# Attention over the 32 best keys and a feed-forward: values stationary in TensorE, scores in two halves, the mask applied to the scores, the last tokens of two batches merged

## The chip, the core and the metric

The kernel runs on one core of a Trainium2 chip. TensorE (PE) multiplies matrices into PSUM; VectorE (DVE), ScalarE (ACT) and GpSimd (POOL) work on tiles of 128 partitions, GpSimd on SBUF alone; SyncE (SP) issues most of the DMAs. The metric is the device time in microseconds of one execution.

## The reference, cut to what matters

```
B, H, S, D = 8, 8, 576, 64
scores = scale * matmul(q, k^T)                      # 576 x 576 for each of 64 heads
kth    = the 32nd largest of each row
scores = where(scores >= kth, scores, -1e9)
attn   = exp(scores - max);  attn /= sum(attn) + 1e-9
x      = matmul(attn, v)      # (B,H,S,D) -> (4608, 512), the heads side by side
h      = x @ w_in             # 512 -> 2048
out    = (h - tanh(h)) @ w_out  # 2048 -> 512
```

All is float32; the weights arrive as float64 words and are rounded to float32 in the kernel.

## The kernel before, in words

The 576 queries of a batch are four blocks of 128 and a remainder of 64. A *step* is two score tiles of 128 rows and 576 columns: one block of queries in two heads or, for the remainder, 64 queries in four heads, two stacked in a tile. A batch has 18 steps, 16 full and 2 of the remainder; the whole run has 144. Steps go block by block, and in a block through the heads.

For each step four things happen, in three neighbouring rounds of the loop at L378. `scores` (L177) multiplies on TensorE: a matmul of 512 keys and one of 64 for a head, then the same for the other head. Two heads share a tile of 128 partitions, so one head's operands lie on partitions 0 to 63 and the other's on 64 to 127. ScalarE copies the result to `sc` (L191). `top` (L194) finds the 32 largest of each row on VectorE in four rounds: MAX8 takes eight (L202), MATCH_REPLACE strikes them out (L213). After the first round ScalarE already forms the exponentials `e` (L208). After the last, GpSimd compares the scores with the 32nd largest (L216) and multiplies the result into `e` (L219). `weigh` (L221) transposes `e` on TensorE (L227, L233), has ScalarE copy it to `et`, and multiplies it with the values (L247): `et` is stationary, 128 queries wide, and 64 values with a column of ones move, which gives the row sums too.

When all heads of a block are done, `seam` (L262) divides by the sums and transposes the block into `xT` (L281), which is 320 or 256 tokens wide: a *unit* is blocks 0 and 1 of a batch, or 2, 3 and the remainder. The feed-forward of a unit is 64 matmuls with w_in (L298), sixteen tanh (L306) and subtractions (L308), and 16 matmuls of 512 columns with w_out for each block (L318); the remainder's 64 tokens are a block of their own. The source deals this work out over the steps, some 10% faster than it comes in.

Each engine runs its instructions in a fixed order, which a scheduler writes when the program is built: it does not keep the order of the source but moves instructions of neighbouring steps past one another where no data forbid it. PSUM holds one set of scores (four banks), two banks for transposes and values (`zt_ps`), two for the feed-forward (`h_ps`). In the first 13 rounds the weights are converted, 32 pieces of four VectorE, two ScalarE and two GpSimd instructions (L106 to L126). In the built program each matmul of the source is two instructions on TensorE, each transpose one.

Of the kernel before, what the change touches and what calls it, by code (L numbers as in the profile page):

```python
# [14 lines left out]
NEG = -3.0e38  # L15
TOP = 32
# [4 lines left out]
class Block:  # L21
# [3 lines left out]
    def __init__(self, b, qt, H):  # L25
        self.b, self.qt = b, qt
        self.rem = qt == J
        tiles = [(h, h + 1) for h in range(0, H, 2)] if self.rem else [(h,) for h in range(H)]
        self.pairs = [tiles[i : i + 2] for i in range(0, len(tiles), 2)]
        self.xs = None  # L30


class Unit:
    """The tokens of some blocks of one batch, which go through the feed-forward together."""

    def __init__(self, b, qts):
        self.b, self.qts = b, qts
        self.xT = None
        self.g = {}
# [3 lines left out]
def kernel(  # L43
# [16 lines left out]
    DE = D + 1  # L60
# [5 lines left out]
    assert CD == FJ == 4 and DFF // WJ == DM == 512  # L66
    assert D == 64 and R == 64 and DM == H * D
# [8 lines left out]
    ldpool = pool("ld", 2)  # L76
    kqpool = pool("kq", 5)
    scpool = pool("sc", 2)
    wpool = pool("w", 3)
    mpool = pool("m", 16)  # L80
    epool = pool("e", 2)
    etpool = pool("et", 2)
    xpool = pool("x", 2)
    hpool = pool("h", 2)
# [14 lines left out]
    def load_weights(j, i):  # L99
        """Piece i of quarter j (w_in's, then w_out's)."""  # L100
# [8 lines left out]
        # the mantissa: 1 + (its upper 20 bits + its lower 32 bits / 2^32) / 2^20  # L109
# [5 lines left out]
        # the power of two, 0 below float32's range and infinite above it, and the sign  # L115
# [13 lines left out]

    raw, kT, qT, vb = {}, {}, {}, {}  # L130

    def load_rows(dst, src, b, hp):
        for hh in range(2):
            h = 2 * hp + hh
            nc.sync.dma_start(
                dst(slice(0, P), slice(0, J), hh),
                src[b, h, 0:JP, :].rearrange("(p j) d -> p j d", j=J),
            )
            nc.sync.dma_start(dst(slice(0, R), J, hh), src[b, h, JP:S, :])

    def load_kq(b, hp):
        for name, src in (("k", k), ("q", q)):
            t = ldpool.tile([P, J + 1, 2, D], FP32, tag=f"{name}in", name=f"{name}in")
            load_rows(lambda p, j, hh, t=t: t[p, j, hh, :], src, b, hp)
            raw[name, b, hp] = t

    def load_v(b, hp):
        t = kqpool.tile([P, 2, J + 1, DE], FP32, tag="vb", name="vb")
        nc.gpsimd.memset(t[:, :, :, D:DE], 1.0)
        load_rows(lambda p, j, hh: t[p, hh, j, 0:D], v, b, hp)  # L150
        vb[b, hp] = t

    def turn_kq(b, hp):
        for name, dst in (("k", kT), ("q", qT)):
            t = raw.pop((name, b, hp))
            d = dst[b, hp] = kqpool.tile([P, S], FP32, tag=f"{name}T", name=f"{name}T")
            ps = zt_ps.tile([P, 512], FP32, tag="zt", name="kqps")
            for c in range(J):
                nc.tensor.transpose(
                    ps[:, c * P : (c + 1) * P], t[:, c, :, :].rearrange("p h d -> p (h d)"), ident[:]  # L160
                )
            nc.scalar.copy(d[:, 0:JP], ps[:])
            ps = zt_ps.tile([P, 512], FP32, tag="zt", name="kqps")
            nc.tensor.transpose(
                ps[:, 0:R], t[0:R, J, :, :].rearrange("p h d -> p (h d)"), ident[0:R, 0:R]
            )
            nc.scalar.copy(d[:, JP:S], ps[:, 0:R])
# [210 lines left out]
    for n in range(-5, NS + 2):  # L378
        if 0 <= n + 1 < NS:
            scores(n + 1, *steps[n + 1])  # L380
# [51 lines left out]
```

## Time and profile before

| | |
|---|---|
| median of 3 runs | 2315.93 us (2315.67 to 2323.74) |
| the profiled execution, its span (first to last instruction); no other time of it is given | 2319.4 us |
| TensorE matmuls busy | 2118.6 us, 91% |
| VectorE busy | 1630.6 us, 70% |
| GpSimd busy | 1035.6 us, 45% |
| ScalarE busy | 862.4 us, 37% |

Times of a stretch count from the start of the span. A matmul's busy time includes a tail in which the next one already runs, so the pace of a series, its length over its count, is what an instruction costs TensorE; the mean duration is longer. PE rows name the part of the array used, rows x columns: 64*128 is half of its rows.

### The profile page before, as it was taken

The page shows a single profiled execution, that of the slowest core. Times are in us where ns is not written, and L with a number is a line of the kernel's source. Part 1 is how long each engine was busy: PE and PEld are TensorE (multiplying, and loading weights), DVE is VectorE, ACT ScalarE, POOL GpSimd, SP SyncE. Part 2 cuts the span into 40 slices and gives each one's busy share as a digit, 9 for nine tenths or more (in the row PEclk, how much of TensorE's full clock was granted, in tenths as well). Part 3 has the DMA queues.
Part 4 walks back from the last instruction along what each step waited for, and adds up shares of the span by engine and source line. Part 5 has one row for each costly group of instructions (what it writes and reads, how often), then busy time and mean ns, then how long its engine had stood idle before and what let it go on. Part 6 is the DMA issues. An engine that isn't in the chain of part 4 may idle for free.

```text
span 2319.4 us, 26938 instructions
## 1 busy us (share of the span) xinstructions
PE 2118.6 (91%) x9728; PEld 1355.2 (58%) x9728; DVE 1630.6 (70%) x3304; ACT 862.4 (37%) x1825; POOL 1035.6 (45%) x614
## 2 busy tenths in 40 slices
PE   5546688999989999999989999999989999999989
PEld 2334545656656575656656575656556575656654
DVE  5877785767758777777668677767758777767720
ACT  4333333434344344434344344434344344434320
POOL 5656553444434434444434434444434444444420
PEclk6555886999979999999979999999979999999989
DMA  6111102000020001100020001100020001000000
GB/s 166 48 55 55 37 23 50 17 10 3 16 56 1 9 3 43 29 10 3 15 56 1 10 3 46 26 10 3 16 56 1 10 3 38 8 6 7 5 5 12
DMA packets 126724, 56.27 MB, mean 24 GB/s; under 512 B 117888, under 2 KB 117888, under 8 KB 126592
## 3 DMA queue, kind: packets, MB, share of 16 engines
q1 hardware_dynamic: 121984, 37.78, 6.6%
q10 hardware_dynamic: 4608, 16.78, 2.2%
q8 instruction: 77, 1.26, 0.2%
q14 instruction: 55, 0.45, 0.1%
HBM read 45.09 MB, written 9.44 MB: 24 GB/s over the span
## 4 chain that ended last, share of the span: by engine, by line
PE 72%; POOL 10%; DVE 10%; issue 5%; ACT 2%; DMA 1%; SPq 0%; POOLq 0%; ACTq 0%
PE ops L318 24%; PE hps L298 20%; PE av L247 13%; PE scps L183 8%; DVE w L213 4%; PE zt L227 4%; DVE m L202 4%; POOL sc L216 3%; POOL e L219 3%; POOL f L120 2%; ACT sc L191 2%; PE zt L233 1%; DVE f L123 1%; PE xtps L281 1%; DMA kin<-in_k_dram 1%
## 5 line engine op out<-in xcount | busy, mean ns | idle before, releaser
L216 POOL TENSOR_SCALAR sc<-sc,m 128x576 f32<-128x576 f32 x288 | 500.1, 1747 | 986.9 <-DVE m L202 914.5
L202 DVE MAX8 m<-w 128x8 f32<-128x576 f32 x864 | 614.0, 747 | 0.0
L318 PE MATMUL ops<-w_out,g 128*128 128x512 f32 (+1 forms) x1280 | 593.0, 604 | 3.4 <-POOL w_out L126 3.4
L298 PE MATMUL hps<-xT,w_in 128*128 128x320 f32 (+1 forms) x2048 | 549.2, 422 | 6.2 <-DVE g L308 5.1
L298 PEld LDWEIGHTS hps<-xT,w_in 128*128 128x128 f32 x2048 | 393.0, 197 | 125.1 <-issue 20.8
L247 PEld LDWEIGHTS av<-vb,et 128*128 128x128 f32 (+3 forms) x3200 | 400.6, 191 | 98.7 <-issue 22.4
L247 PE MATMUL av<-vb,et 128*128 128x65 f32 (+3 forms) x3200 | 445.1, 284 | 14.0 <-ACT et L230 11.7
L213 DVE MATCH_REPLACE8 w<-m,w 128x576 f32<-128x576 f32 x576 | 427.7, 742 | 0.0
L202 DVE MAX8 m<-sc 128x8 f32<-128x576 f32 x288 | 204.4, 748 | 283.0 <-ACT sc L191 283.0
L219 POOL TENSOR_TENSOR e<-e,sc 128x1152 f32<-128x1152 f32 x144 | 378.7, 2630 | 11.9
L318 PEld LDWEIGHTS ops<-w_out,g 128*128 128x128 f32 (+1 forms) x1280 | 218.3, 181 | 252.9 <-issue 240.9
L183 PE MATMUL scps<-kT,qT 64*128 64x64 f32 (+3 forms) x1280 | 324.9, 480 | 10.9 <-ACT sc L191 10.5
L227 PE MATMUL zt<-ident,e 128*128 128x128 f32 x1152 | 176.5, 300 | 119.2 <-POOL e L219 110.4
L191 ACT COPY sc<-scps 128x1152 f32<-128x1152 f32 x144 | 161.4, 1121 | 326.9 <-PE scps L183 267.9
L306 ACT ACTIVATE th<-hps 128x256 f32<-128x256 f32 (+1 forms) x256 | 105.2, 411 | 372.0 <-PE hps L298 351.3
L183 PEld LDWEIGHTS scps<-kT,qT 64*128 64x128 f32 (+1 forms) x1280 | 139.9, 190 | 160.3 <-issue 132.7
L308 DVE TENSOR_TENSOR g<-hps,th 128x256 f32<-128x256 f32 (+1 forms) x256 | 114.9, 449 | 157.0 <-ACT th L306 156.6
L208 ACT ACTIVATE e<-sc,nb 128x576 f32<-128x576 f32 x288 | 220.8, 775 | 4.2 <-ACT nb L207 0.2
L227 PEld LDWEIGHTS zt<-ident,e 128*128 128x128 f32 x1152 | 138.6, 152 | 133.6 <-POOL e L219 114.9
L213 DVE MATCH_REPLACE8 w<-m,sc 128x576 f32<-128x576 f32 x288 | 211.8, 742 | 0.0
L230 ACT COPY et<-zt 128x512 f32<-128x512 f32 x288 | 157.2, 596 | 13.6 <-PE zt L227 13.5
L255 ACT COPY xs<-av 128x130 f32<-128x130 f32 x144 | 40.2, 279 | 240.6 <-PE av L247 206.7
(45 smaller groups left out, 833.7 us busy)
## 6 DMA issues: line engine op xcount, KB each, us to landing
kin<-in_k_dram SPq DMA_DIRECT2D x64, 128.0 KB, 2.5
raw<-in_moe_w_in_dram ACTq DMA_DIRECT2D x16, 512.0 KB, 4.0
qin<-in_q_dram SPq DMA_DIRECT2D x64, 128.0 KB, 2.5
vb<-in_v_dram SPq DMA_DIRECT2D x64, 128.0 KB, 2.6
raw<-in_moe_w_out_dram ACTq DMA_DIRECT2D x16, 512.0 KB, 3.5
out_dram<-ot SPq DMA_DIRECT2D x32, 256.0 KB, 2.3
kin<-in_k_dram SPq DMA_DIRECT2D x64, 16.0 KB, 2.3
qin<-in_q_dram SPq DMA_DIRECT2D x64, 16.0 KB, 2.3
```

Source lines behind the costliest of these rows:

```text
L183: nc.tensor.matmul(ps[i * R : i * R + ql, ti, s0:s1], qT[g.b, hp][r, g.qt * P : g.qt * P + ql], kT[g.b, hp][r, s0:s1], start=True, stop=True,)
L191: nc.scalar.copy(sc[:], ps[:, :, 0:S])
L202: nc.vector.max(m[ti][:], cur[ti])
L208: nc.scalar.activation(e[:, ti, :], sc[:, ti, :], AF.Exp, bias=nb[:], scale=scale)
L213: nc.vector.match_replace(w[:], m[ti][:], cur[ti], NEG)
L216: nc.gpsimd.tensor_scalar(sc[:, ti, :], sc[:, ti, :], m[ti][:, 7:8], None, ALU.is_ge)
L219: nc.gpsimd.tensor_tensor(e[:], e[:], sc[:], ALU.mult)
L227: nc.tensor.transpose(zt[:, c * P : (c + 1) * P], e[:, ti, c * P : (c + 1) * P], ident[:])
L230: nc.scalar.copy(et[:, ti, 0:J, :], zt[:].rearrange("p (c j) -> p c j", c=J))
L247: nc.tensor.matmul(av[0:ql, nh * DE : (nh + 1) * DE], et[rows, ti, c, i * R : i * R + ql], vb[g.b, hp][rows, h % 2, c, :], start=(c == 0), ...
L298: nc.tensor.matmul(ps[:, 0:N], w_in[j][:, c, fo : fo + P], u.xT[:, c, 0:N], start=(c == 0), stop=(c == CD - 1),)
L318: nc.tensor.matmul(acc[u, qt][0:ql, :], u.g[f][:, o : o + ql], w_out[part][:, f % FJ, :], start=(f == 0), stop=(f == CF - 1),)
```

## The change

Each head pair is now done for two blocks of queries at a time: a batch's steps run through blocks 0 and 1 of the four head pairs, then through blocks 2 and 3, with a remainder step after every second pair. The parts:

- *Scores.* The 576 keys go in two halves of 288. Within a half the two heads follow each other, so the partitions (rows of the array) alternate. The second head's keys are stored with the last 64 first, so that the last 64 of both heads lie side by side in the tile of weights.
- *Mask.* After the search GpSimd forms two numbers per row and head; ScalarE computes a Relu that is 0 for a score among the 32 largest and huge otherwise, GpSimd subtracts it from the scores, and ScalarE takes the exponential of that, which also adds up the row sums. All of it comes after the last round of the search.
- *Weights.* The last 64 keys of both heads are transposed together: nine transposes for ten.
- *Values.* The values (128 keys x 64) are stationary and the transposed weights of two blocks (256 queries) move, so the result comes out transposed, one head in partitions 0 to 63 of `av` (the first 64 columns of the array), the other in 64 to 127. The reciprocals of the sums are spread over 64 columns on GpSimd, transposed on TensorE (`rb`), copied by ScalarE, and VectorE multiplies them into `xT`. `seam` goes.
- *Units.* Blocks 0 and 1, or blocks 2 and 3; in every second batch the second unit also takes the last 64 tokens of two batches as one block, 384 tokens in all.

```diff
+BIG = 2.0**80
...
-    ldpool = pool("ld", 2)
-    kqpool = pool("kq", 5)
+    ldpool = pool("ld", 1)
+    kqpool = pool("kq", 4)
...
+        x = vb[b, hp] = kqpool.tile([P, 2, J, D], FP32, tag="vb", name="vb")
+        y = vr[b, hp] = kqpool.tile([P, D], FP32, tag="vr", name="vr")
+        for t in range(2):
+            h = 2 * hp + t
+            nc.sync.dma_start(x[:, t, :, :], main_rows(v, b, h))
+            nc.sync.dma_start(y[half(t), :], v[b, h, JP:S, :])
...
+            for rows, o in [(half(0), 0), (half(1), R)] if name == "k" else [(slice(0, P), 0)]:
+                nc.scalar.copy(d[rows, o : o + JP], ps[rows, :])
+                o = 0 if o else JP
+                nc.scalar.copy(d[rows, o : o + R], p4[rows, 0:R])
...
+        ps = sc_ps.tile([P, 2, 2, 512], FP32, tag="sc", name="scps")
+        for s in range(2):
+            ks = slice(s * S2, (s + 1) * S2)
+            for i in range(2 if g.rem else 1):
+                qs = slice(JP, S) if g.rem else slice(g.qt * P, (g.qt + 1) * P)
+                rows = half(i) if g.rem else slice(0, P)
+                for t in range(2):
                     nc.tensor.matmul(
-                        ps[i * R : i * R + ql, ti, s0:s1],
-                        qT[g.b, hp][r, g.qt * P : g.qt * P + ql],
-                        kT[g.b, hp][r, s0:s1],
+                        ps[rows, t, s, 0:S2],
+                        qT[g.b, g.hp + i][half(t), qs],
+                        kT[g.b, g.hp + i][half(t), ks],
                         start=True,
                         stop=True,
                     )
-        sc = scpool.tile([P, 2, S], FP32, tag="sc", name="sc")
-        nc.scalar.copy(sc[:], ps[:, :, 0:S])
+        sc = scpool.tile([P, 2, 2, S2], FP32, tag="sc", name="sc")
...
         rounds = TOP // 8
         for i in range(rounds):
-            m = [mpool.tile([P, 8], FP32, tag="m8", name="m8") for _ in range(2)]
-            for ti in range(2):
-                nc.vector.max(m[ti][:], cur[ti])
-            if i == 0:
-                e = epool.tile([P, 2, S], FP32, tag="e", name="e")
-                for ti in range(2):
-                    nb = mpool.tile([P, 1], FP32, tag="nb", name="nb")
-                    nc.scalar.mul(nb[:], m[ti][:, 0:1], -scale)
-                    nc.scalar.activation(e[:, ti, :], sc[:, ti, :], AF.Exp, bias=nb[:], scale=scale)
-                st[n]["e"] = e
+            m8 = slice(8 * i, 8 * i + 8)
+            for t in range(2):
+                nc.vector.max(m[:, t, m8], cur[t])
             if i < rounds - 1:
-                for ti in range(2):
+                for t in range(2):
                     w = wpool.tile([P, S], FP32, tag="w", name="w")
-                    nc.vector.match_replace(w[:], m[ti][:], cur[ti], NEG)
-                    cur[ti] = w[:]
-        for ti in range(2):
-            nc.gpsimd.tensor_scalar(
-                sc[:, ti, :], sc[:, ti, :], m[ti][:, 7:8], None, ALU.is_ge
+                    nc.vector.match_replace(w[:], m[:, t, m8], cur[t], NEG)
+                    cur[t] = w[:]
+        nb = mpool.tile([P, 2], FP32, tag="nb", name="nb")
+        nc.gpsimd.tensor_scalar(nb[:], m[:, :, 0], -scale, None, ALU.mult)
+        tb = mpool.tile([P, 2], FP32, tag="tb", name="tb")
+        nc.gpsimd.tensor_scalar(tb[:], m[:, :, TOP - 1], BIG, None, ALU.mult)
+        z = zpool.tile([P, 2 * S], FP32, tag="z", name="z")
+        zv = z[:].rearrange("p (t k) -> p t k", t=2)
+        den = mpool.tile([P, 2], FP32, tag="den", name="den")
+        for t in range(2):
+            nc.scalar.activation(zv[:, t, :], scf[:, t, :], AF.Relu, bias=tb[:, t : t + 1], scale=-BIG)
+        nc.gpsimd.tensor_tensor(zv, scf, zv, ALU.subtract)
+        for t in range(2):
+            nc.scalar.activation(
+                zv[:, t, :],
+                zv[:, t, :],
+                AF.Exp,
+                bias=nb[:, t : t + 1],
+                scale=scale,
+                accum_out=den[:, t : t + 1],
             )
-        nc.gpsimd.tensor_tensor(e[:], e[:], sc[:], ALU.mult)
...
+            et, e4, rd = ets[g.hp]
+            rd = rd[:, g.qt % 2, :]
+        for t in range(2):
             zt = zt_ps.tile([P, 512], FP32, tag="zt", name="zt")
+            m0 = t * (S + R)
             for c in range(J):
                 nc.tensor.transpose(
-                    zt[:, c * P : (c + 1) * P], e[:, ti, c * P : (c + 1) * P], ident[:]
+                    zt[:, c * P : (c + 1) * P], z[:, m0 + c * P : m0 + (c + 1) * P], ident[:]
                 )
-            nc.scalar.copy(et[:, ti, 0:J, :], zt[:].rearrange("p (c j) -> p c j", c=J))
+            nc.scalar.copy(et[:, t, :, o : o + P], zt[:].rearrange("p (c j) -> p c j", c=J))
         zt = zt_ps.tile([P, 512], FP32, tag="zt", name="zt")
-        for ti in range(2):
-            nc.tensor.transpose(zt[0:R, ti * P : (ti + 1) * P], e[:, ti, JP:S], ident[:])
-        nc.scalar.copy(
-            et[0:R, :, J, :], zt[0:R, 0 : 2 * P].rearrange("p (t j) -> p t j", t=2)
-        )
+        nc.tensor.transpose(zt[:, 0:P], z[:, JP : JP + P], ident[:])
+        nc.scalar.copy(e4[:, o : o + P], zt[:, 0:P])
...
+        nc.gpsimd.tensor_scalar(rd, den[:], EPS, None, ALU.add)
+        return ets.pop(g.hp) if o else None
...
+        ri = xpool.tile(list(rd.shape), FP32, tag="ri", name="ri")
+        nc.vector.reciprocal(ri[:], rd[:])
+        rx = xpool.tile([P, 2, 2, D], FP32, tag="rx", name="rx")
+        nq = 1 if g.rem else 2
+        nc.gpsimd.tensor_copy(rx[:, 0:nq], ri[:].unsqueeze(3).to_broadcast([P, nq, 2, D]))
+        N = P if g.rem else 2 * P
         av = zt_ps.tile([P, 512], FP32, tag="zt", name="av")
+        for i in range(2 if g.rem else 1):
+            cols = half(i) if g.rem else slice(0, N)
+            hp = g.hp + i
+            for c in range(J + 1):
+                for t in range(2):
+                    rows = slice(0, P) if c < J else half(t)
                     nc.tensor.matmul(
+                        av[half(t), cols],
+                        vb[g.b, hp][:, t, c, :] if c < J else vr[g.b, hp][rows, :],
+                        et[:, t, c, cols] if c < J else e4[rows, cols],
                         start=(c == 0),
                         stop=(c == J),
                     )
+        rb = zt_ps.tile([P, 512], FP32, tag="zt", name="rb")
+        for i in range(nq):
+            nc.tensor.transpose(
+                rb[:, i * P : (i + 1) * P], rx[:, i].rearrange("p t d -> p (t d)"), ident[:]
+            )
+        rs = xpool.tile([P, 2 * P], FP32, tag="rs", name="rs")
+        nc.scalar.copy(rs[:, 0:N], rb[:, 0:N])
+        if g.rem:
+            u = units[g.b | 1, 1]
+            for i in range(2):
+                o = 2 * P + (g.b % 2) * R
+                nc.vector.tensor_tensor(
+                    xt(u)[:, g.hp + i, o : o + R], av[:, half(i)], rs[:, half(i)], ALU.mult
+                )
+        else:
+            u = units[g.b, g.qt // 2]
+            nc.vector.tensor_tensor(xt(u)[:, g.hp, 0:N], av[:, 0:N], rs[:, 0:N], ALU.mult)
...
+        for a in range(2):
+            blocks = [block(b, 2 * a), block(b, 2 * a + 1)]
+            if a and b % 2:
+                blocks.append(rem_block(b - 1))
+            units[b, a] = Unit(f"{b}{a}", blocks)
+            for hp in range(NHP):
+                steps += [Step(b, hp, 2 * a), Step(b, hp, 2 * a + 1)]
+                if a and hp % 2:
+                    steps.append(Step(b, hp - 1, J))
+            done[len(steps) - 1] = units[b, a]
...
+            n = first[b] + 2 * hp
+            at(n - 6, lambda b=b, hp=hp: load_kq(b, hp))
+            at(n - 4, lambda b=b, hp=hp: turn_kq(b, hp))
+            at(n - 2, lambda b=b, hp=hp: load_v(b, hp))
...
```

The scheduler's order of TensorE, of one step in the feed-forward's first product, before (`scps` scores, `zt` transposed weights, `av` values, `hps` feed-forward; x is how often in a row, counted in matmuls of the source):

```order
L298 MATMUL hps<-xT,w_in_107 128x320 x8
L183 MATMUL scps<-kT,qT 128x512
L183 MATMUL scps<-kT,qT 128x64
L183 MATMUL scps<-kT,qT 128x512
L183 MATMUL scps<-kT,qT 128x64
L227 MATMUL zt<-ident,e 128x128 x8
L298 MATMUL hps<-xT,w_in_107 128x320 x2
L233 MATMUL zt<-ident,e 64x128 x2
L247 MATMUL av<-vb,et 128x65 x10
L298 MATMUL hps<-xT,w_in_107 128x320 x6
```

The same place of the change, with the scores of a step parted once, and `rb`, the transposed reciprocals:

```order
L189 MATMUL scps<-kT,qT 128x288
L329 MATMUL hps<-xT,w_in_111 128x256 x8
L189 MATMUL scps<-kT,qT 128x288 x3
L262 MATMUL zt<-ident,z 128x128 x8
L329 MATMUL hps<-xT,w_in_112 128x256 x2
L267 MATMUL zt<-ident,z 128x128
L329 MATMUL hps<-xT,w_in_112 128x256
L291 MATMUL av<-et,vb 64x256 x8
L291 MATMUL av<-e_8547,vr 64x256 x2
L300 MATMUL rb<-ident,rx 128x128 x2
```

The values stand once in two steps, behind the last transposes of the second, and the two heads' matmuls alternate in them.

ScalarE's order around a step with tanh (`th`), before (`nb` and `e` are the exponentials' offset and the exponentials):

```order
L306 ACTIVATE th<-hps 128x256 x5
L191 COPY sc<-scps 128x1152
L230 COPY et<-zt 128x512 x2
L207 ACTIVATE nb<-m_7495 128x1
L234 COPY et<-zt 64x2x128
L208 ACTIVATE e<-sc,nb 128x576
L207 ACTIVATE nb<-m_7496 128x1
L208 ACTIVATE e<-sc,nb 128x576
L255 COPY xs<-av 128x130
```

And of the change (the Relus write `z` from `sc` and `tb`, the exponentials `z` and `den`):

```order
L197 COPY sc<-scps 128x1152
L265 COPY et<-zt 128x4x128 x2
L225 ACTIVATE z<-sc,tb 128x576 x2
L268 COPY e_6653<-zt 128x128
L228 ACTIVATE z,den<-z,nb 128x576 x2
L304 COPY rs<-rb 128x256
L337 ACTIVATE th<-hps 128x256 x5
```

The exponentials stood behind the first maximum of their own step; now Relus and exponentials stand behind the last, and the tanh behind both.

## Rows read from the trace of the kernel before

**Rows 1.** The page: span, and busy us (share of the span) of TensorE.
```profile
span 2319.4 us, 26938 instructions
PE 2118.6 (91%) x9728; PEld 1355.2 (58%) x9728; DVE 1630.6 (70%) x3304; ACT 862.4 (37%) x1825; POOL 1035.6 (45%) x614
```

**Rows 2.** Three stages: stretch, length, busy us of each engine, granted clock, DMA.
```profile
core 0: us, PE busy (x) PEld busy (x) DVE busy (x) ACT busy (x) POOL busy (x), PEclk, DMA share, GB/s
26.00:376.00 350.00, 228.84 (x890) 147.02 (x888) 270.03 (x491) 122.13 (x247) 204.95 (x116) 0.67 0.18 54
376.00:2210.00 1834.00, 1783.36 (x8451) 1145.98 (x8449) 1330.68 (x2759) 713.22 (x1522) 809.15 (x473) 0.96 0.07 17
2210.00:2319.40 109.40, 95.40 (x354) 55.73 (x354) 17.64 (x38) 16.12 (x36) 8.59 (x7) 0.91 0.02 6
```

**Rows 3.** Groups of instructions, 376 to 2209.4 us, VectorE: first maxima.
```profile
L202 DVE MAX8 m<-sc 128x8 f32<-128x576 f32 x250 | 177.1, 748 | 271.9 <-ACT sc L191 271.9
```

**Rows 4.** Waits of the whole run: us in total, times, longest us.
```profile
DVE g L308 <- ACT th L306: 156.6, 98, 8.0
...
DVE f L123 <- POOL f L120: 65.7, 28, 5.5
```

**Rows 5.** TensorE in order of time: start us, us, what, how many.
```profile
1141.89 2.16 PE L183 MATMUL scps<-kT,qT 64*64 64x512 f32 x16
...
1235.89 1.30 PE L183 MATMUL scps<-kT,qT 64*128 64x512 f32 x8
...
1252.58 1.12 PE L183 MATMUL scps<-kT,qT 64*128 64x512 f32 x2 [0.26 <-ACT sc L191]
...
1319.80 7.03 PE L318 MATMUL ops<-w_out,g 128*64 128x512 f32 x16
...
1327.00 2.77 PE L247 MATMUL av<-vb,et 128*128 128x65 f32 x20
...
1341.62 7.61 PE L298 MATMUL hps<-xT,w_in 128*128 128x256 f32 x34
...
2215.99 3.53 PE L247 MATMUL av<-vb,et 128*64 128x65 f32 x40
...
2238.10 36.22 PE L298 MATMUL hps<-xT,w_in 128*128 128x320 f32 x128 [0.46 <-ACT xT L284]
```

**Rows 6.** TensorE, 376 to 2210 us, lines L183, L247, L318, L233 one by one.
```profile
376.00:2210.00 1834.00, 255.46 (x1112) 0.96 0.07 17
376.00:2210.00 1834.00, 370.93 (x2780) 0.96 0.07 17
376.00:2210.00 1834.00, 515.08 (x1120) 0.96 0.07 17
376.00:2210.00 1834.00, 51.28 (x251) 0.96 0.07 17
```

**Rows 7.** Groups of instructions, whole run: busy us, mean ns | idle before.
```profile
L298 PEld LDWEIGHTS hps<-xT,w_in 128*128 128x128 f32 x2048 | 393.0, 197 | 125.1 <-issue 20.8 <-DVE g L308 7.0 <-ACT xT L284 2.2
L208 ACT ACTIVATE e<-sc,nb 128x576 f32<-128x576 f32 x288 | 220.8, 775 | 4.2 <-ACT nb L207 0.2
L308 DVE TENSOR_TENSOR g<-hps,th 128x256 f32<-128x256 f32 x128 | 52.9, 415 | 44.5 <-ACT th L306 44.1
L233 PEld LDWEIGHTS zt<-ident,e 128*64 128x64 f32 x288 | 23.9, 113 | 90.8 <-ACT et L230 49.4 <-issue 23.2 <-ACT nb L207 14.4
L265 POOL TENSOR_SCALAR rden<-xs 128x8 f32<-128x8 f32 x32 | 7.8, 243 | 87.1 <-ACT xs L255 86.3
L267 DVE RECIPROCAL rinv<-rden 128x8 f32<-128x8 f32 x32 | 6.5, 203 | 39.5 <-POOL rden L265 39.5
```

**Rows 8.** GpSimd in order of time, the mask of one step.
```profile
1349.51 3.42 POOL L216 TENSOR_SCALAR sc<-sc,m 128x576 f32<-128x576 f32 x2 [14.80 <-DVE m L202]
1353.02 2.63 POOL L219 TENSOR_TENSOR e<-e,sc 128x1152 f32<-128x1152 f32 x1
```

More of the change, by code (lines that the diff above doesn't have):

```diff
@@ L18, with __init__ @@
 J = 4
[L21 to L26 removed]
+class Step:
+    def __init__(self, b, hp, qt):
+        self.b, self.hp, self.qt = b, hp, qt
         self.rem = qt == J
[L28 to L30 removed]
 class Unit:
[L36 to L37 removed]
+    def __init__(self, name, blocks):
+        self.name, self.blocks = name, blocks
+        self.N = 128 * len(blocks)
         self.xT = None
@@ L59 @@
     R = S - JP
-    DE = D + 1
+    S2 = S // 2
     CD = DM // P
@@ L243, in weigh @@
-        for ti, heads in enumerate(g.pairs[pi]):
-            for i, h, hp, r in heads_of(heads):
-                for c in range(J + 1):
-                    rows = slice(0, P if c < J else R)
+        nc.tensor.transpose(zt[:, 0:P], z[:, JP : JP + P], ident[:])
+        nc.scalar.copy(e4[:, o : o + P], zt[:, 0:P])
+        if g.rem:
+            rd = xpool.tile([P, 1, 2], FP32, tag="rdr", name="rdr")
+            nc.gpsimd.tensor_scalar(rd[:, 0, :], den[:], EPS, None, ALU.add)
+            return et, e4, rd
@@ L327, in ffn_o, with block, rem_block @@
         ot = hpool.tile([P, DM], FP32, tag="ot", name="ot")
[L328 to L334 removed]
+        nc.scalar.copy(ot[:], acc.pop((u, i))[:])
+        for rows, dst in u.blocks[i]:
+            nc.sync.dma_start(dst, ot[rows, :])
     def ffn(u):
[L337 removed]
         for f in range(CF):
[L339 to L340 removed]
+            yield CD * u.N, lambda f=f: ffn_h(u, f)
+        for i in range(len(u.blocks)):
             for part in range(WJ):
[L342 removed]
+                yield FJ * DM, lambda i=i, part=part: ffn_o(u, i, part)
+    def block(b, qt):
+        return [(slice(0, P), out[b * S + qt : b * S + qt + JP : J, :])]
+    def rem_block(b):
+        return [(half(i), out[(b + i) * S + JP : (b + i + 1) * S, :]) for i in range(2)]
     units = {}
[L348 to L349 removed]
+    steps, first, done = [], [], {}
     for b in range(B):
         first.append(len(steps))
[L352 to L356 removed]
+        for a in range(2):
[8 more added lines that the diff above has]
+            done[len(steps) - 1] = units[b, a]
     NS = len(steps)
[L358 to L359 removed]
+    share = 1.1 * B * S * 2 * CF * CD / NS
     todo = {}
@@ L377 @@
     credit = 0.0
-    for n in range(-5, NS + 2):
+    for n in range(-6, NS + 2):
         if 0 <= n + 1 < NS:
-            scores(n + 1, *steps[n + 1])
+            scores(n + 1, steps[n + 1])
         if 0 <= n < NS:
@@ L383 @@
         if 0 <= n - 1 < NS:
-            g, pi = steps[n - 1]
-            weigh(n - 1, g, pi)
-            if pi == len(g.pairs) - 1:
-                u = units[g]
-                seam(g, u)
-                if g.qt == u.qts[-1]:
-                    work += list(ffn(u))
+            g = steps[n - 1]
+            ready = weigh(n - 1, g)
+            st.pop(n - 1)
+            if ready:
+                values(g, *ready)
+            if n - 1 in done:
+                work += list(ffn(done[n - 1]))
         for fn in todo.pop(n, []):
```

165 lines of the change are left out of this document (54 added, 111 removed).

## The prediction

> **What bounds the kernel now.** I read the busy shares first, then the span cut into three stages, then who waits for whom, then TensorE in order of time. TensorE is busy for 2118.6 of 2319.4 us [rows 1]. The stages say more than that mean [rows 2]. From 26 to 376 us (the first 18 steps, with the weights being converted) VectorE is the busiest, 270 of 350 us, and the granted clock averages 0.67. From 376 to 2210 us TensorE is busy for 1783 of 1834 us, 97%, at clock 0.96; VectorE for 1331 us, 73%. From 2210 us on only the last unit's feed-forward is left. The middle stage holds 125 steps, since 250 first maxima of two heads each fall into it [rows 3]: 14.67 us a step, of which TensorE works 14.27 and VectorE 10.65. So in the stage that makes up four fifths of the time TensorE decides, and VectorE's long wait for the score copies, 271.9 us [rows 3], is the picture of an engine kept waiting by TensorE. What the change is worth there is the TensorE time that it takes away, until VectorE at some 11 us a step becomes the limit.
>
> **TensorE's paces.** 34 feed-forward matmuls of 256 moving columns take 7.61 us, 0.224 each; 16 of 512 columns take 7.03, 0.44 each [rows 5]. So a matmul instruction costs 0.87 ns per moving column, and each matmul of the source is two instructions. The value matmuls move 65 columns, which by that would be 0.057 us, yet 20 of them take 2.77 us, 0.139 each [rows 5]: they pay for loading 128 stationary columns and not for what they move. The scores of a step move 2304 columns in eight instructions, 2.0 us by that pace, but where the eight stand together they take 1.30 [rows 5]: the two heads sit on different halves of the rows of the array and run beside each other.
>
> **The change, part by part (middle stage).**
>
> *Scores.* They take 255.5 us there [rows 6], 14 of the steps being remainder steps at 2.16 us [rows 5]; the other 111 take (255.5 - 30.2) / 111 = 2.03 us, since the 512 and 64 of one head come before the other head's and the scheduler puts other work between them, as where two 512s stand alone for 1.12 us [rows 5]. After, the moved columns are the same 2304, but the heads alternate every 288, so that neighbours always lie on different rows. I take today's best, 1.30, for all: 111 x 0.73 = 81 us less. Bounds: nothing, if splits go on costing as now (the order of the change still parts a step's four matmuls in places), and 95 us if the remainder steps, whose four combinations of halves now follow each other, also fall from 2.16 to about 1.2.
>
> *Values.* 370.9 us there [rows 6]. Now a pair of heads and two blocks of queries need ten matmuls, 20 instructions, each of 64 stationary and 256 moving columns. One after another they cost 20 x 0.224 = 4.5 us for two steps, which were 2 x 2.77; 55.5 such pairs make 249 us, and 14 remainder steps of 40 short instructions at most the 3.53 us of today [rows 5], 49 us: 298, so 73 us less. But the two heads write to different halves of the columns of the array and alternate. If these halves run beside each other as the row halves do, it is 2.4 us a pair and about 1.9 a remainder step, 160 us: 211 us less. No row of before shows two matmuls on the same rows and different columns, so both ends stay; I take the second, for halves of rows do it in [rows 5], and the remainder scores, on different rows and columns, also take 2.16 us where their 4608 columns would need 4.0.
> The Trainium skill speaks for this end (TensorEngine Tiling, Performance Considerations): with a free dimension of 64 on the right it advises swapping stationary and streaming sides and tiling two columns wide. Another page speaks against it: TensorE: Matmul & The Clock Gate, Part 3 (The mechanism) says that a weight load overlaps running matmuls only where its row group differs, and all of these share their rows. Feed-forward loads share their rows too, take 0.197 us each [rows 7] and vanish in a pace of 0.224, so the trace disagrees; by that rule 16 loads of 0.113 [rows 7] would come on top, 1.8 us a pair and 100 us in the stage.
>
> *Output matmuls.* The remainder's 64 queries of two batches share one block: 576 matmuls for 640. A tenth of 515.1 us [rows 6] is 52 us. The first feed-forward product moves the same columns in all.
>
> *Transposes.* One of 128 columns instead of two narrow ones a step: of 51.3 us [rows 6] I take 20 off, since the fixed tail stays. The transposes of x (four a block) go, those of the reciprocals (two a pair of steps) come: nothing.
>
> *Sum on TensorE:* 81 + 52 + 20 + 211 = 364, or 226 with the values one after another. 1783 becomes 1419 or 1557 us: 11.4 or 12.5 us a step.
>
> *VectorE.* 80 reciprocals for 40 at 0.203, and 96 multiplies out of PSUM of at most the 0.415 of the subtraction of 256 columns [rows 7]: 42 us in all, 0.3 a step: 10.95.
>
> *GpSimd and ScalarE.* GpSimd loses two comparisons of 1.71 a step [rows 8] and gains three tiny operations of some 0.24 [rows 7]; it stays far below the others. ScalarE gains two Relu passes, taken as the 0.775 of the exponential [rows 7]: 862 + 223 = 1085 us in all, 54% of the forecast. What counts is the chain from the last maximum to the transposes. Now it is two comparisons and a product on GpSimd, 3.42 + 2.63 us [rows 8], with the exponentials done early, after the first maximum. Then it is two tiny operations, two Relus, a subtraction of 2.63 and two exponentials: 0.5 + 1.55 + 2.63 + 1.55 = 6.2 us. As long, but ScalarE now stands in it twice, and the tanh that VectorE's subtractions need stand behind the exponentials in ScalarE's order. Today's cover is that TensorE is late anyway. With both engines near 11 us a step that cover is thin, so I put 0.9 us a step on top of the larger figure: 11.4 + 0.9 = 12.3, an estimate, between 0.1 (the chain all hidden) and 2.5 (0.4 of it on the path).
>
> *The ends.* In the first stage VectorE's 270 us stay; GpSimd's comparisons, which stand in front of the weight conversion there (65.7 us of waits of VectorE [rows 4]), go. I take 330 for 350, bounds 290 and 365. At the end the last unit has 384 columns for 320: 36.2 us of matmuls [rows 5] become 43.5, so 109 becomes about 118.
> Forecast: 26 + 330 + 125 x 12.3 + 118 = 2011 us on the trace's clock. The profiled execution spans 2319.4 us, 3.5 over the median of 2315.93, within the runs; the forecast for the median is 2010.
>
> **Rivals.**
> *Column halves take turns.* The values then cost 298 us and TensorE stays the bound at 12.5, with 0.4 of idle time: 26 + 330 + 125 x 12.9 + 118 = 2087. For it: nothing before shows the halves side by side. Against: the row halves.
> *All hidden.* The chain costs nothing and the step is 11.5: 26 + 320 + 1438 + 117 = 1901. For it: TensorE reached 97% in this stage. Against: at 73% VectorE always had room, which now goes.
> *The chain lands on VectorE (slower).* In a step of feed-forward, ScalarE waits at the Relus for VectorE and at the exponentials for GpSimd; the tanh queued behind come late, VectorE waits for them in the middle of the next search, and TensorE, with two PSUM buffers for the product, stops after two units. It decides the sign from 14.67 - 10.95 = 3.7 us of wait a step on, 60% of the 6.2 us chain; at 5 us a step it is 26 + 360 + 125 x 16 + 125 = 2511. For it: ScalarE's order, shown with the change. Against: tanh also stand between and before, and GpSimd's share of the chain shrinks.
>
> **Chances.** Forecast 0.48 (own range 1950 to 2055), turns 0.27, all hidden 0.15, chain 0.06, and 0.04 for something between 2150 and the present. Within 0.5%, about what a measurement here cannot tell from no change, lie 0.02; slower 0.07; faster 0.91. The range runs from all hidden to beyond the turns with more waits: 1895 to 2160.
>
> **What would show it.** Scores: eight instructions of 288 together in about 1.3 us. Values: 20 instructions of 256 columns in 2.4 us (side by side) or 4.5 (turns). Output matmuls: 1152 instructions for 1280. TensorE busy 1420 to 1560 us in the stretch of the last 125 searches, and VectorE's share up from 73% to near 90%. The chain rival would show as VectorE's subtractions waiting for tanh for over 450 us in total, 156.6 now [rows 4]. The forecast is wrong if the step falls by less than a microsecond, or if the clock of the middle stage drops well below 0.96 since TensorE pauses oftener: at 0.67, as in the first stage, the saving in columns would be given back.

## The result and the profile after

The change takes 2199.22 us, median of 4 runs (2194.36 to 2205.01), against 2317.8 for before (now 4 runs): a ratio of 0.948 (95% interval 0.946 to 0.950). Faster, as forecast, but by 119 us and not by 306; the time lies outside the range of 1895 to 2160. The profiled execution took 2196.8 us and spans 2195.0.

The three stages of the changed kernel, in the columns of [rows 2]; again 125 searches begin in the middle one:

```profile
core 0: us, PE busy (x) PEld busy (x) DVE busy (x) ACT busy (x) POOL busy (x), PEclk, DMA share, GB/s
24.60:355.60 331.00, 184.27 (x745) 106.49 (x743) 244.46 (x503) 137.18 (x275) 173.98 (x135) 0.70 0.19 57
355.60:2083.70 1728.10, 1511.09 (x7084) 873.23 (x7083) 1347.76 (x2877) 829.27 (x1732) 434.95 (x569) 0.95 0.07 18
2083.70:2195.00 111.30, 95.12 (x302) 49.91 (x299) 21.89 (x46) 19.79 (x41) 7.02 (x9) 0.92 0.02 7
```

The ends came out near the forecast (331 for 330, 111 for 118 us), the first of them by luck, as shown further down. The middle stage did not: 13.82 us a step for 12.3. TensorE works 1511 us, 272 less than before, and VectorE 1348; neither fills the 1728. TensorE now stands still for 217 us, where in [rows 2] it was 51.

TensorE's lines in that stage, for L183, L247 and L318 of [rows 6]: scores (L189), values (L291), output (L347), and then the first product (L329), whose columns in the whole run did not change:

```profile
355.60:2083.70 1728.10, 200.10 (x1112) 0.95 0.07 18
355.60:2083.70 1728.10, 189.63 (x1680) 0.95 0.07 18
355.60:2083.70 1728.10, 464.55 (x992) 0.95 0.07 18
355.60:2083.70 1728.10, 492.46 (x1786) 0.95 0.07 18
```

The scores fell by 55 us, the values by 181, the output by 51. The first product rose by 17 us, though some 1.7% fewer of its columns fall into this stage (1396 instructions of 256 columns and 390 of 384, for 896 of 320 and 896 of 256); its row of before (L298):

```profile
376.00:2210.00 1834.00, 475.89 (x1792) 0.96 0.07 17
```

Where TensorE waits is seen best in one stretch. TensorE in order of time (start us, us, what, and in brackets the pause before it):

```profile
1349.02 0.33 PE L267 MATMUL zt<-ident,z 128*128 128x128 f32 x1
1349.50 1.95 PE L291 MATMUL av<-et,vb 128*64 128x256 f32 x16 [0.16 <-ACT et L265]
1353.13 0.65 PE L291 MATMUL av<-e,vr 64*64 64x256 f32 x4 [1.68 <-ACT e L268]
1353.71 0.44 PE L300 MATMUL rb<-ident,rx 128*128 128x128 f32 x2
1353.98 7.89 PE L347 MATMUL ops<-w_out,g 128*128 128x512 f32 x18
1361.80 1.24 PE L189 MATMUL scps<-kT,qT 64*128 64x288 f32 x8
1362.97 1.09 PE L262 MATMUL zt<-ident,z 128*128 128x128 f32 x8
1363.90 1.03 PE L329 MATMUL hps<-xT,w_in 128*128 128x256 f32 x4
1366.93 0.33 PE L267 MATMUL zt<-ident,z 128*128 128x128 f32 x1 [2.00 <-ACT etr L265]
```

ScalarE, in the same stretch:

```profile
1351.30 0.78 ACT L228 ACTIVATE z<-z,nb 128x576 f32<-128x576 f32 x1 [1.85 <-POOL z L226]
...
1352.07 0.76 ACT L228 ACTIVATE z<-z,nb 128x576 f32<-128x576 f32 x1
...
1352.83 0.24 ACT L268 COPY e<-zt 128x128 f32<-128x128 f32 x1
...
1363.28 0.77 ACT L228 ACTIVATE z<-z,nb 128x576 f32<-128x576 f32 x1 [2.79 <-POOL z L226]
...
1364.52 0.78 ACT L228 ACTIVATE z<-z,nb 128x576 f32<-128x576 f32 x1
...
1365.29 1.10 ACT L197 COPY sc<-scps 128x1152 f32<-128x1152 f32 x1
1366.29 1.08 ACT L265 COPY etr<-zt 128x512 f32<-128x512 f32 x2
```

VectorE's next search:

```profile
1366.42 1.42 DVE L210 MAX8 m<-sc 128x8 f32<-128x576 f32 x2 [7.72 <-ACT sc L197]
```

ScalarE stands still before an exponential until GpSimd has subtracted. Behind it in ScalarE's order waits a copy of 0.24 us (1352.83), which the last value matmuls need: TensorE pauses 1.68 us, has 18 instructions of the output product to do after them, and comes to the next scores only at 1361.80. Then ScalarE is held again before an exponential; the score copy, ready to be made at 1363.0, is made at 1365.29, and VectorE has waited 7.72 us for its next search. In this stretch the chain of the mask and TensorE's work have come to stand one behind the other.

### The profile page after: what moved, and what is told of

Read it like the earlier page. It is cut to its first block, busy times and chain, and to the rows that moved or that the text cites. A ratio compares the mean times of both kernels' runs of the same rounds, so it can differ in the third digit from the quotient of the medians.

```text
span 2195.0 us, 24121 instructions
## 1 busy us (share of the span) xinstructions
PE 1799.9 (82%) x8160; PEld 1035.6 (47%) x8160; DVE 1624.4 (74%) x3440; ACT 997.5 (45%) x2069; POOL 628.4 (29%) x726
## 5 line engine op out<-in xcount | busy, mean ns | idle before, releaser
L347 PE MATMUL ops<-w_out,g 128*128 128x512 f32 x1152 | 537.4, 609 | 19.2 <-DVE g L339 9.6
L226 POOL TENSOR_TENSOR z<-sc,z 128x1152 f32<-128x1152 f32 x144 | 381.1, 2647 | 205.8 <-issue 153.8
L329 PE MATMUL hps<-xT,w_in 128*128 128x256 f32 x1536 | 392.7, 401 | 54.9 <-DVE g L339 40.5
L225 ACT ACTIVATE z<-sc,tb 128x576 f32<-128x576 f32 x288 | 208.7, 768 | 328.9 <-POOL tb L219 328.7
L228 ACT ACTIVATE z<-z,nb 128x576 f32<-128x576 f32 x288 | 220.9, 768 | 286.9 <-POOL z L226 286.9
L329 PEld LDWEIGHTS hps<-xT,w_in 128*128 128x128 f32 x1536 | 291.7, 201 | 115.2 <-DVE g L339 57.6
L347 PEld LDWEIGHTS ops<-w_out,g 128*128 128x128 f32 x1152 | 214.9, 197 | 233.0 <-issue 206.3
L262 PE MATMUL zt<-ident,z 128*128 128x128 f32 x1152 | 178.3, 299 | 147.5 <-ACT z L228 143.0
L189 PE MATMUL scps<-kT,qT 64*128 64x288 f32 (+1 forms) x1280 | 247.4, 458 | 3.7 <-ACT sc L197 3.7
L339 DVE TENSOR_TENSOR g<-hps,th 128x256 f32<-128x256 f32 (+1 forms) x256 | 113.8, 451 | 108.4 <-ACT th L337 106.7
L329 PE MATMUL hps<-xTb,w_in 128*128 128x384 f32 x512 | 186.5, 507 | 7.9 <-DVE g L339 7.2
L189 PEld LDWEIGHTS scps<-kT,qT 64*128 64x128 f32 (+1 forms) x1280 | 117.2, 186 | 114.8 <-issue 87.9
L291 PE MATMUL av<-et,vb 128*64 128x256 f32 x1024 | 143.9, 430 | 9.4 <-ACT et L265 9.3
```

The source lines that it names most:

```text
L189: nc.tensor.matmul(ps[rows, t, s, 0:S2], qT[g.b, g.hp + i][half(t), qs], kT[g.b, g.hp + i][half(t), ks], start=True, stop=True,)
L225: nc.scalar.activation(zv[:, t, :], scf[:, t, :], AF.Relu, bias=tb[:, t : t + 1], scale=-BIG)
L226: nc.gpsimd.tensor_tensor(zv, scf, zv, ALU.subtract)
L228: nc.scalar.activation(zv[:, t, :], zv[:, t, :], AF.Exp, bias=nb[:, t : t + 1], scale=scale, accum_out=den[:, t : t + 1],)
L262: nc.tensor.transpose(zt[:, c * P : (c + 1) * P], z[:, m0 + c * P : m0 + (c + 1) * P], ident[:])
L291: nc.tensor.matmul(av[half(t), cols], vb[g.b, hp][:, t, c, :] if c < J else vr[g.b, hp][rows, :], et[:, t, c, cols] if c < J else e4[rows, ...
```

## The experiments

The first four ask whether the mask's chain costs the time.

**Early exponentials.**

```diff
+            if i == 0:
...
+                    nc.scalar.mul(nb[:, t : t + 1], m[:, t, 0:1], -scale)
+                    nc.scalar.activation(
+                        zv[:, t, :], scf[:, t, :], AF.Exp, bias=nb[:, t : t + 1], scale=scale
+                    )
...
-            nc.scalar.activation(zv[:, t, :], scf[:, t, :], AF.Relu, bias=tb[:, t : t + 1], scale=-BIG)
-        nc.gpsimd.tensor_tensor(zv, scf, zv, ALU.subtract)
...
+            nc.gpsimd.tensor_scalar(scf[:, t, :], scf[:, t, :], m[:, t, TOP - 1 : TOP], None, ALU.is_ge)
+        nc.gpsimd.tensor_tensor(zv, zv, scf, ALU.mult)
...
+            nc.scalar.activation(
+                m[:, t, :], m[:, t, :], AF.Exp, bias=nb[:, t : t + 1], scale=scale,
+                accum_out=den[:, t : t + 1],
+            )
```

> The change with the mask of before put back: the exponentials follow the first maximum, GpSimd compares and multiplies after the last, and the row sums come from 32 exponentials of the maxima, one round later. Theory chain: the time went to the mask's chain, which now passes twice through ScalarE behind the last maximum and holds back the score and weight copies queued behind it; without it TensorE's pauses of the middle stage (217 us) fall to the 55 of before, and the whole takes 2030 to 2080 us. Rival TensorE: its own work (12.1 us a step, not 11.4) and the order of the big feed-forward pieces set the time: 2170 to 2200 us. Rival GpSimd: the longer GpSimd chain (6.05 us for 2.63) costs as much as ScalarE's waits: 2200 or more.

Measured: 2237.14 us, 0.964 of before (0.961 to 0.966), slower than the change. By itself this spoke for the GpSimd rival. Its waits (us in total, times, longest) told otherwise:

```profile
POOL sc L226 <- DVE m L210: 879.2, 137, 12.1
ACT m L238 <- POOL sc L226: 553.3, 246, 8.2
```

ScalarE was held by GpSimd once more (407 of the 553 us between 400 and 1900 us), by the experiment's own fault: the small exponentials overwrote maxima that GpSimd's comparison still read.

**No subtraction.**

```diff
-        nc.gpsimd.tensor_tensor(zv, scf, zv, ALU.subtract)
-                scale=scale,
+                scale=-(2.0**-80),
```

> The change without GpSimd's subtraction (the exponentials are taken of the scaled Relu, so the weights are other numbers): the chain is 2.6 us shorter, ScalarE does not wait between Relu and exponential. Theory chain: ScalarE's 255 us of waits for the subtraction go and most of the step's 1.7 us of TensorE pause with them: 2050 to 2110 us. Rival TensorE: within 20 us of the change, 2180 to 2200.

Measured: 1962.74 us, 0.846 (0.844 to 0.847): 236 us below the change, more than the chain theory asked for. TensorE's 1453.84 busy us in a middle stage of 1528.30 leave 74 us of pauses, and the clock rises to 0.99:

```profile
327.30:1855.60 1528.30, 1453.84 (x7089) 853.17 (x7087) 1337.54 (x2883) 826.60 (x1734) 108.27 (x444) 0.99 0.08 21
```

The step is 12.2 us, what the forecast had for the change itself. Two waits of ScalarE in the change, from 356 to 2084 us:

```profile
ACT z L228 <- POOL z L226: 255.2, 122, 3.1
ACT z L225 <- POOL tb L219: 244.5, 103, 6.5
```

The first, before the exponentials, is what this run takes away. The second, before the Relus, is as long here (243.0 us from 400 to 1900 us) and leaves TensorE with 74 us of pauses: a wait of the same length costs far less there.

**Subtraction by heads.**

```diff
-        nc.gpsimd.tensor_tensor(zv, scf, zv, ALU.subtract)
+        for t in range(2):
+            nc.gpsimd.tensor_tensor(zv[:, t, :], scf[:, t, :], zv[:, t, :], ALU.subtract)
```

> The change with the subtraction done for each head by itself, so that the first exponential can start after the first half: some 1.3 us off ScalarE's wait a step. Theory chain: 2110 to 2160 us. Rival TensorE: 2185 to 2205.

Measured: 2136.55 us, 0.921 (0.919 to 0.923), as the chain theory had it. ScalarE's wait before the exponentials falls from 255 to 130 us in the middle stage, TensorE's pauses from 217 to 179.

**Values head by head.**

```diff
-            for c in range(J + 1):
-                for t in range(2):
+            for t in range(2):
+                for c in range(J + 1):
```

> The change with all ten value matmuls of one head ahead of those of the other, so that column halves do not alternate. TensorE's values then cost some 130 us more of its time in the whole run (20 instructions of 0.22 for a pair instead of 2.6 us). Rival TensorE, TensorE as the bound: 2310 to 2330 us. Theory chain: TensorE's pauses take up a part, 2230 to 2280 us. If the halves run beside each other all the same, as the parted scores of before did in places, within 10 us of the change.

Measured: 2312.86 us, 0.997 (0.996 to 0.998): 114 above the change, in the TensorE rival's range. TensorE in order of time, for the first row of the stretch above:

```profile
1420.90 1.94 PE L291 MATMUL av<-et,vb 128*64 128x256 f32 x8
```

Eight instructions of one head take what 16 of two alternating heads take, so the halves do run beside each other in the change, and only if they alternate. The middle stage:

```profile
359.00:2196.10 1837.10, 1676.03 (x7078) 963.76 (x7078) 1349.23 (x2878) 831.23 (x1732) 435.51 (x569) 0.94 0.07 17
```

TensorE works 165 us longer than in the change and its pauses fall from 217 to 161 us, so the pauses swallow a third of the longer work; the other two thirds are added to the time.

The next four ask how the chain costs it: by what ScalarE has queued behind, or by its length.

**Mask written late.**

```diff
+        st[n].update(scf=scf, m=m)
+
+    def mask(n):
+        scf, m = st[n]["scf"], st[n]["m"]
         nb = mpool.tile([P, 2], FP32, tag="nb", name="nb")
...
             if n - 1 in done:
                 work += list(ffn(done[n - 1]))
+        if 0 <= n < NS:
+            mask(n)
```

> The change with the mask (Relu, subtraction, exponentials) of a step written after the weights and values of the step before it, instead of ahead of them: the same instructions and the same chain, 6.2 us long, but ScalarE's three copies of weights mostly stand ahead of the Relus now. Theory queue: what costs is that copies stand behind exponentials that wait for GpSimd, so that TensorE's values, the feed-forward behind them and the next scores come late: 2060 to 2130 us. Rival length: the length of the chain itself is on the path, as the runs with a shorter one suggest, whatever stands behind it: 2170 to 2210.

Measured: 2217.18 us, 0.956 (0.955 to 0.958), 7 us above the range of either theory. The queue theory, in this form, fell: the copies of weights mostly stood ahead of the Relus now, but ScalarE still waited 246 us for GpSimd in the middle stage (255 in the change), and other work stood behind the exponentials: the copies of reciprocals (`rs`) and of scores, and the tanh. One place, ScalarE and then TensorE:

```profile
1408.57 0.77 ACT L232 ACTIVATE z<-z,nb 128x576 f32<-128x576 f32 x1 [2.79 <-POOL z L230]
...
1409.34 0.35 ACT L308 COPY rs<-rb 128x256 f32<-128x256 f32 x1
...
1409.74 0.66 PE L164 MATMUL kqps<-ident,kin 128*128 128x128 f32 x4 [2.92 <-ACT rs L308]
```

**Late, and by heads.** Both edits above.

> The mask written late and the subtraction done head by head, both together. Theory queue: little over the late mask alone, 2040 to 2110 us, and below the per-head run's 2137. Rival length: as the per-head run, 2120 to 2150.

Measured: 2150.9 us, 0.927 (0.926 to 0.929), at the upper edge of the length rival's range: the subtraction by heads helps as before (66 us, 63 without the late mask), the late mask does not.

**Three quarters of the first product.**

```diff
-        for c in range(CD):
+        for c in range(CD - 1):
```

> The change without the last of the four partial products with w_in (the result is another one): some 135 us less of TensorE's time, 10 us less in a step with the first product, the chain untouched. If TensorE's work and the chain stand in series, as queue and length both have it now that making the values longer by 130 us cost 114: 2070 to 2110 us. If the chain alone sets the pace: 2170 to 2200.

Measured: 2073.68 us, 0.894 (0.893 to 0.896), 126 less than the change, as the series reading had it. The middle stage:

```profile
351.50:1971.00 1619.50, 1430.10 (x6631) 797.28 (x6630) 1340.14 (x2877) 830.12 (x1729) 435.39 (x570) 0.94 0.08 20
```

It is 109 us shorter: TensorE works 81 us less and pauses 28 us less. Nothing of the work taken away turned into waiting, so on this side TensorE and chain stand in series.

**The kernel before, with the new mask alone.**

```diff
-                    nc.scalar.activation(e[:, ti, :], sc[:, ti, :], AF.Exp, bias=nb[:], scale=scale)
...
-            nc.gpsimd.tensor_scalar(
-                sc[:, ti, :], sc[:, ti, :], m[ti][:, 7:8], None, ALU.is_ge
-            )
-        nc.gpsimd.tensor_tensor(e[:], e[:], sc[:], ALU.mult)
...
+            nc.scalar.activation(
+                e[:, ti, :], sc[:, ti, :], AF.Relu, bias=tb[:, ti : ti + 1], scale=-BIG
+            )
+        nc.gpsimd.tensor_tensor(e[:], sc[:], e[:], ALU.subtract)
+        for ti in range(2):
+            nc.scalar.activation(
+                e[:, ti, :], e[:, ti, :], AF.Exp, bias=nb[:, ti : ti + 1], scale=scale
+            )
```

> The kernel before with the change's mask alone (Relu, subtraction and exponentials after the last maximum; the rest as before). Queue: the copies and tanh of before then stand behind it too; TensorE's 55 us of pauses in the middle stage grow to some 150 to 250, 2400 to 2520 us. Length: the chain is as long as before (6.2 for 6.05 us), so within 30 us of before, 2300 to 2350.

Measured: 2496.13 us, 1.077 (1.075 to 1.080): 176 us over before, though the chain is no longer than before's. So length alone is not it. Only part of this is pauses:

```profile
357.80:2381.10 2023.30, 1917.19 (x8450) 1229.57 (x8448) 1334.26 (x2759) 848.66 (x1526) 476.93 (x723) 0.90 0.06 16
```

TensorE's pauses grew to 106 us; its busy time grew by 134 with the same instructions, at a granted clock of 0.90 for 0.96. Rows of one place show how:

```profile
1102.92 2.79 PE L325 MATMUL ops<-w_out,g 128*64 128x512 f32 x6
1107.18 0.41 PE L240 MATMUL zt<-ident,e 128*64 128x128 f32 x2 [1.47 <-ACT et L237]
1107.66 4.67 PE L254 MATMUL av<-vb,et 128*128 128x65 f32 x20
...
1127.49 0.41 PE L240 MATMUL zt<-ident,e 128*64 128x128 f32 x2 [1.39 <-ACT et L237]
...
1128.17 2.76 PE L254 MATMUL av<-vb,et 128*128 128x65 f32 x20
```

And the engines' busy time and the granted clock in two stretches around the first pause:

```profile
1100.00:1107.00 7.00, 5.71 (x24) 2.31 (x22) 4.85 (x11) 4.23 (x6) 3.40 (x5) 1.00 0.00 0
1107.00:1114.00 7.00, 6.75 (x24) 4.55 (x24) 4.29 (x10) 1.25 (x4) 0.00 (x0) 0.58 0.00 1
```

After a pause of 1.47 us the 20 value matmuls take 4.67 us, for 2.77 in [rows 5]; the granted clock falls from 1.00 to 0.58, so most of that stretch ran at the lower of its two levels, 1.2 GHz. Here the pause is paid twice. Not every pause is: after the one of 1.39 us, 20 value matmuls take 2.76 us, and in the first stretch of the change shown above, with pauses of 1.68 and 2.00 us, the granted clock is 1.00:

```profile
1349.00:1367.00 18.00, 14.17 (x63) 7.16 (x63) 8.65 (x18) 7.76 (x17) 6.03 (x7) 1.00 0.04 15
```

The last four ask what about the chain it is.

**Early exponentials, sums apart.** The edit against the first early run:

```diff
+        ex = xpool.tile([P, 2, TOP], FP32, tag="ex", name="ex")
...
-                m[:, t, :], m[:, t, :], AF.Exp, bias=nb[:, t : t + 1], scale=scale,
+                ex[:, t, :], m[:, t, :], AF.Exp, bias=nb[:, t : t + 1], scale=scale,
```

> The early exponentials again, but the 32 small ones for the sums write to a tile of their own; in the earlier run they wrote over the maxima, and ScalarE waited 407 us for GpSimd's comparison to have read them. GpSimd's chain after the last maximum is 6.05 us, and ScalarE has no part in it. Theory held ScalarE: what costs is ScalarE standing in the middle of the chain, so that everything queued on it waits for GpSimd; without it 2030 to 2090 us. Theory length: a chain of 6 us costs the same whichever engine it is on: 2180 to 2240.

Measured: 2083.23 us, 0.897 (0.896 to 0.899). Against the first early run one operand differs, and 154 us go with it. GpSimd's chain is the same 6.05 us; ScalarE is no longer held by it, and the wait of 553 us is gone (the small exponentials now wait 303 us for VectorE's maxima, which come first):

```profile
POOL sc L226 <- DVE m L210: 785.6, 135, 11.5
ACT ex L239 <- DVE m L210: 303.1, 175, 6.6
```

So ScalarE held by GpSimd costs, at the same length of chain. The length is not free either: TensorE still pauses for 127 us in the middle stage here (1605 us, of which it works 1478), 68 of them in transposes that wait for GpSimd's product.

**One fused instruction on VectorE.** The edit against the run just above:

```diff
-            nc.gpsimd.tensor_scalar(scf[:, t, :], scf[:, t, :], m[:, t, TOP - 1 : TOP], None, ALU.is_ge)
-        nc.gpsimd.tensor_tensor(zv, zv, scf, ALU.mult)
+            nc.vector.scalar_tensor_tensor(
+                out=zv[:, t, :], in0=scf[:, t, :], scalar=m[:, t, TOP - 1 : TOP], in1=zv[:, t, :],
+                op0=ALU.is_ge, op1=ALU.mult,
+            )
```

> Early exponentials, and comparison and product as one instruction a head on VectorE instead of three on GpSimd: the chain is 1.4 us, neither GpSimd nor ScalarE is in it, and VectorE has 1.4 us more a step (12.3 us). Both theories: TensorE's pauses fall to 80 us or less; VectorE nearly sets the step, 12.5 to 13: 2030 to 2090 us. If pauses stay, neither holds.

Measured: 1995.94 us, 0.860 (0.858 to 0.862), the fastest of all that leave nothing out, and below the 2030 to 2090 expected.

```profile
335.80:1877.50 1541.70, 1466.51 (x7077) 857.87 (x7074) 1510.04 (x3130) 786.97 (x1980) 63.04 (x195) 0.97 0.08 21
```

VectorE is now busy for 1510 of 1542 us: it is the bound. TensorE pauses for 75 us, as expected, and its 1467 us are near what its work comes to with few pauses (1454 in the run without the subtraction). The run is 87 us faster than the one above, where ScalarE was free of GpSimd as well: that much goes with GpSimd's three instructions, their time or their place, though VectorE took the work over.

**Subtraction on VectorE.**

```diff
-        nc.gpsimd.tensor_tensor(zv, scf, zv, ALU.subtract)
+        nc.vector.tensor_tensor(zv, scf, zv, ALU.subtract)
```

> The change with the subtraction on VectorE, some 1.2 us for GpSimd's 2.63: the chain is 1.4 us shorter, but VectorE's own order now holds a wait for the Relus, with its next search behind it. Theory held ScalarE and length alike: 2080 to 2140 us. Rival: VectorE's wait for the Relus, 1.8 us a step in front of its next search, costs as much as it gives: 2180 to 2230.

Measured: 2044.48 us, 0.881 (0.880 to 0.882), better than any theory had it, though VectorE has 1.35 us more in a step. ScalarE still stands in the middle of the chain, but waits 92 us there for VectorE in the middle stage, for 255 for GpSimd in the change.

**Subtraction on both.**

```diff
-        nc.gpsimd.tensor_tensor(zv, scf, zv, ALU.subtract)
+        for t in range(2):
+            (nc.vector if t else nc.gpsimd).tensor_tensor(zv[:, t, :], scf[:, t, :], zv[:, t, :], ALU.subtract)
```

> The subtraction of the first head on GpSimd and of the second on VectorE, side by side: 1.3 us for 2.63. Held ScalarE and length: below the per-head run, 2060 to 2130 us. Rival (VectorE held by the Relus): 2150 to 2200.

Measured: 2107.96 us, 0.909 (0.907 to 0.910), within the expectation, and 63 us above the run with the whole subtraction on VectorE. Why is not shown: ScalarE's wait for GpSimd before the exponentials, 72 us in the middle stage, is shorter than its wait for VectorE in that run (92), so the sum of this wait alone does not set the time.

## Why the prediction was wrong

*TensorE's paces: right.* Eight score instructions take 1.24 us, as forecast from the eight of [rows 5]. 20 value instructions take 1.95 + 0.65 us beside each other (forecast 2.4; 4.5 in turns). The Trainium skill's advice to swap the sides and tile two columns wide (TensorEngine Tiling, Performance Considerations) holds here: 16 instructions in 1.95 us, 8 in 1.94 when the halves do not alternate. The Trainium skill's rule that weight loads overlap running matmuls only where the row group differs (TensorE: Matmul & The Clock Gate, Part 3, The mechanism) does not show here: these 16, each with a weight load of its own, share their rows and take 0.12 us each.

*The sum on TensorE: a little too large.* 364 us were forecast, 272 came, 11.4 us a step against 12.1. With most of the pauses gone it is 1467 us, 11.7 (the fused run, which keeps 75 us of pauses), or 1454 (the run without the subtraction). So 1467 - 1419 = 48 us, or 35, are terms reckoned too large. Scores and values in the fused run's middle stage:

```profile
335.80:1877.50 1541.70, 199.43 (x1110) 0.97 0.08 21
335.80:1877.50 1541.70, 174.61 (x1680) 0.97 0.08 21
```

The scores thus gave 56 us and not 81, since the scheduler still parts some steps' four matmuls, the values 196 and not 211; the last transposes 12 and not 20. The reciprocals' transposes cost 6 more than those of x had and the first product 8 more, where the sum had nothing; against that the output product gave 63 and not 52. The other 1511 - 1467 = 45 us come with the pauses, the same instructions taking longer: the values 15 us, the output product 13, the first product 9. The granted clock of the stage is 0.95 in the change and 0.97 in the fused run; how much of the 45 us is its doing was not separated. The forecast named the clock only as a danger and gave it no price.

*The allowance for the chain: the step that failed.* The prediction put 0.9 us a step on top of TensorE's work, because the chain was "as long" as before's and the engines' cover merely thin. Measured: 1728 - 1511 = 217 us of pauses, 1.74 a step, and the 45 us above. Of the middle stage's 191 us too much (1728 - 1537), 99 are pauses (217 less the 118 that the forecast held above TensorE's 1419), 45 come with them, 48 are TensorE's terms. So it was the price that failed. The length of the chain was reckoned rightly, but for the 0.19 us by which each exponential's sum is read out; that ScalarE stands in it twice was named and given no price of its own:

```profile
L228 ACT ACTIVATION_READ_ACCUMULATOR z<-z,nb 128x1 f32 x288 | 53.8, 187 | 0.0
L228 ACT ACTIVATE z<-z,nb 128x576 f32<-128x576 f32 x288 | 220.9, 768 | 286.9 <-POOL z L226 286.9
```

The second row has the main cause: 286.9 us of the whole run in which ScalarE, the engine that here empties PSUM for both others, stands before an exponential for GpSimd. Before, its exponentials waited for an early maximum only, and the 6.05 us on GpSimd held, in the middle stage, the transposes one round later for 13.8 us and the score copies for 26.8. What this hold costs at an equal length of chain is seen between the two early runs, with one operand between them: 154 us. The Trainium skill says of ScalarE that it is strictly first in, first out (TensorE: Matmul & The Clock Gate, Part 1, Architectural detail); the trace agrees: in the stretch above, the copy at 1352.83, whose transpose was done at 1349.35, ran only after both exponentials.

*The ends and the signs.* The 331 us of the first stage are luck. The 330 rested on VectorE's 270 us staying and its 65.7 us of waits for GpSimd going; VectorE works 244 us there, and that wait is longer:

```profile
DVE f L125 <- POOL f L122: 78.4, 29, 5.0
```

Of the prediction's own two signs of being wrong, the step that falls by less than a microsecond came (14.67 to 13.82); a much lower clock did not (0.95 for 0.96). The time fell where the prediction had put a chance of 0.04, between 2150 us and the present.

*The rivals.* The slower rival had the right kind of mechanism, ScalarE held in the chain, with the wrong victims: it watched for VectorE's subtractions waiting for tanh, which took 106.7 us and not over 450; the copies of scores and weights were late instead. It also took chain and TensorE as things one of which covers the other, as the forecast did. The values' taking turns and the chain all hidden are refuted by the rows above.

*What stays open.* Why the mask written late costs 18 us more than the change is not settled; a scheduler's order that kept every copy ahead of every waiting exponential was not tried. How the 217 us of pauses divide between ScalarE's hold and the chain's length is not settled either: 127 are left with ScalarE free of GpSimd and 6.05 us on GpSimd, 75 with the fused instruction.

## What to carry to other kernels

When a step is moved behind a slow engine, ask which engine waits in the middle of the new chain and what else it serves; an engine that empties PSUM had better not wait for a slower one. A chain of equal length is no sign of equal cost, and a long wait no sign of a dear one. Once the bound engine is relieved, its work and the chain may add up in the order of instructions, so price the order, not only the sums.

## What the runs showed of the hardware

Half the columns of the array, with all rows shared, run beside each other in float32: 16 alternating instructions of 256 columns in 1.95 us, 8 that do not alternate in 1.94. A subtraction of 128 x 1152 takes GpSimd 2.65 us and VectorE 1.35; one fused comparison and product of 128 x 576 takes VectorE 0.81. TensorE's granted clock fell to its lower level behind one pause of 1.47 us in a stretch where it was otherwise busy, and the price showed up as busy time (4.67 us for 2.77) and not as waiting; behind pauses of 1.39, 1.68 and 2.00 us elsewhere it stayed at 1.00.
